# Products with v for two slots at once, tails' scores in four quadrants, and a gate and a spatial product ordered by their stationary operand

## The chip, the cores and the metric

The program runs on one core of a Trainium2 chip (trn2). The metric is the device time of one execution in microseconds (us). A profile of one execution goes with it. Its engines are PE (matrix products, with PEld for the loads of their stationary operands), DVE (vector), ACT (scalar functions), POOL and SP; SP here only starts DMA transfers. Each engine takes its instructions in the order in which the program lists them.

## What is computed

Attention with rotary position, then a channel mixing block, then a gated block with a spatial product. Cut to what matters (B, H, S, D = 4, 8, 576, 64; DM = 512, DF = 1024):

```python
scores = matmul(rotate(q), rotate(k).T) / sqrt(D)             # per batch and head, 576 x 576
attn = exp(scores - max); attn /= attn.sum() + 1e-9
x = concat_heads(matmul(attn, v))                             # [B, 576, 512]
xk, xr = mix of x and x shifted by one row, with mu_k and mu_r
v2 = square(relu(xk @ w_k)) @ w_v
x = sigmoid(xr @ w_r) * v2
h = relu(x @ w_in); u, g = h[..., :512], h[..., 512:]
g = (g - mean(g)) / sqrt(var(g) + 1e-6)
out = (u * (w_spatial @ g + b_spatial)) @ w_out
```

## The kernel before, in words

Products in fp32 precision are sums of three products of high and low parts (a high times w high, a low times w high, a high times w low) in a type that PE takes in one pass; only the scores are plain fp32, which PE runs as two passes (two records in the trace for each product of the program). The weights with the low parts arrive as 64-bit numbers and are taken apart on ACT, DVE and POOL.

**The first part** (to about 502 us, with a tail that overlaps the second part) is attention and the first block. It is cut into 72 slots, 18 for each batch. A pair is two heads, 64 rows of q and k each, one in partitions 0 to 63 and one in 64 to 127 (`HEAD[0]`, `HEAD[1]`). Slot m of a batch takes 128 queries of one pair (16 slots), or the last 64 queries of two pairs: these are the tails, slots 8 and 9 of a batch. A slot goes through these steps:

- `scores` (line 318, PE): for two halves h of the 576 keys and two heads j, 128 x 288 products into two tiles `ps[0]`, `ps[1]` of PSUM, of which there is one set more. In a tail, pair u = 0 is done first, then u = 1; head j writes partitions `HEAD[j]` of `ps[u]`.
- `top` (L324, DVE), twice: the maximum of a row. `expo` (L329, ACT), twice: the exponential with its sum. `norm` (L334, L335, DVE).
- `high` (L341, ACT) and `low` (L345, DVE), twice each: the probabilities as two fp16 parts, into the tile `p16` (named `p` in the trace), of which there are 3 (`P16S`).
- `turn` (L350, issued by SP): a DMA that transposes `p16` into a tile `pt`, of which there are 3 (`PTS`).
- `values` (L370, PE): 9 pieces of 128 keys, two parts of v, two heads: 36 products of 64 columns of v with 128 queries, the two heads in the two column halves of PE (partitions `HEAD[j]` of one PSUM bank `pv`). A tail has 72 products with 64 queries each.
- `gather` (ACT) copies a `pv` bank out after slots 3, 7, 9, 13 and 17 of a batch, and so makes the input of the block that follows.

For the queries before and after row 256 of each batch the first block runs as `k_dot` (L432, named `mk`), `k_square` and `v_dot` (L462, named `mv`). `prep` loads q, k and v of the next pairs and rotates them (`rope`, L225 and L226, DVE).

The order of this part is made by `Plan`: each step is added with a rank, an engine, a price in us and the steps and buffers that it needs; the planner walks through them and writes, for each engine, the order in which they are issued. The order on the chip is fixed by that, also where a step then waits.

**The second part** (from 502 us) runs batch by batch: `receptance` (product `r`), `gate` (product `hv`, whose stationary operand is the part `x[a]`, 12 products of 512 columns for each 128 rows), `branch` (product `u`, whose stationary operand is the weight), `spatial` (product `sp`, whose stationary operand is the part `vn[a]`) and `project` (product `o`). In `product` each stationary operand is used for two products of 288 columns. `PARTS = (0, 0), (1, 0), (0, 1)` is the order of the parts as (part of the activation, part of the weight). The scheduler of the framework orders this part.

Of the kernel before, what the change touches and what calls it, by code (L numbers as in the profile page):

```python
# [30 lines left out]
RAW, ROT, VVS, PFS, P16S, PTS = 2, 8, 4, 4, 3, 3  # L31
# [65 lines left out]
def body(ctx: ExitStack, tc, qp, kp, vp, cs, mu_k, mu_r, w_k, w_v, w_r, w_in, w_sp, b_sp, w_out, out):  # L97
# [209 lines left out]
    def scores(m):  # L307
        ps = [ps_s.tile([128, 2, 512], F32, tag="s", name=f"s{n}")
              for n in (2 * m, 2 * m + 1)]
        w = which(m)  # L310
        for u in range(2 if w[0][2] == 64 else 1):
            i, c, n, _ = w[u]
            q, k = preps[i][0], preps[i][1]
            for h in range(2):
                for j in range(2):
                    r = HEAD[j]
                    o = ps[u][r, h, :HALF] if n == 64 else ps[j][:, h, :HALF]
                    nc.tensor.matmul(o, q[r, c:c + n], k[r, h * HALF:(h + 1) * HALF], start=True, stop=True)  # L318
        sm = at.tile([128, 4, 2], F32, tag="sm", bufs=4, name=f"sm{m}")
        units[m] = [[x[:, :, :HALF] for x in ps], sm, [None, None], None]  # L320
# [26 lines left out]

    def turn(m):
        pt = at.tile([128, 2, NKC, 128], F16, tag="pt", bufs=PTS, name=f"pt{m}")
        nc.sync.dma_start_transpose(pt.rearrange("p u c q -> p (u c) q"),  # L350
                                    units[m][3].rearrange("p u a b -> p (u a b)"))
        units[m] = pt
# [3 lines left out]
    def values(m):  # L356
        b, w = divmod(m, UN)
        pt = units.pop(m)
# [77 lines left out]
    def k_square(b, h, fc):  # L436
        ps = mo.pop((b, h, "k", fc))[:, :PART[h][1]]
        if fc % 2 == 0:
            mo[b, h, "s"] = moe_tile([128, 2, PART[1][1]], F32, "rl", 2, name=f"rl{b}_{h}_{fc}")[:, :, :PART[h][1]]
        rl = k2 = mo[b, h, "s"]  # L440
# [35 lines left out]
    def moe1(b, h):  # L476

        end = UN * b + (20 if h else 10)
        s, places = end + 1.6, 16 if h else 20
# [18 lines left out]
        for fc in range(NFC):  # L498
            m = at_(fc)
            bank, q, r = ("m", P, fc), fc // 2, ("rl", P, fc // 2)  # L500
            for k in range(2):
                add(m + .1 * k, "PE", .9 * f, lambda fc=fc, k=k: k_dot(b, h, fc, k), ("k", P, fc, k),
                    needs=[("x3", P, 2 * k), ("x3", P, 2 * k + 1)] + [("wlo", c + 4 * (fc // 4)) for c in (2 * k, 2 * k + 1)]
                    + ([("k", P, fc, 0)] if k else last if fc > 3 else []), take=[] if k else [("m", bank)],
                    use=[("x", P)] + ([bank] if k else []))
# [9 lines left out]
        for dc, half in ((0, 0), (1, 0), (0, 1), (1, 1), (2, 0), (2, 1), (3, 0), (3, 1)):  # L515
            m = at_(8 + n)
            n += 1
            for k in (2 * half, 2 * half + 1):
                add(m + .1 * (k % 2), "PE", .9 * f, lambda dc=dc, k=k: v_dot(b, h, dc, k), ("v", P, dc, k),
# [14 lines left out]
    for m in range(N):  # L534
# [3 lines left out]
        add(m - .5, "PE", 1.17, lambda m=m: scores(m), ("s", m), needs=[("rope", *r) for r in rots] + [("s", m - 1)][:m],  # L538
            use=[("rot", *r) for r in rots], take=[("s", ("s", m, 0)), ("s", ("s", m, 1)), ("sm", ("sm", m))])
        for j in range(2):  # L540
            add(m - .4 + .01 * j, "DVE", .71, lambda m=m, j=j: top(m, j), ("top", m, j), needs=[("s", m)], use=[("s", m, j)])
# [9 lines left out]
            needs=[("low", m, 0), ("low", m, 1)] + [("turn", m - 1)][:m], use=[("p16", m)],  # L551
            take=[("pt", ("pt", m))], dma=3.4)
        first = w in (0, 4, 8, 10, 14)
        if first:
            bank = ("pvb", m)
        add(m + 1.5, "PE", 1.15, lambda m=m: values(m), ("pv", m),
            needs=[("turn", m)] + [("vcopy", i) for i in pairs] + ([("pv", m - 1)] if m else []),
            use=[("pt", m)] + [("vv", i) for i in pairs] + ([] if first else [bank]), take=[("pvb", bank)] if first else [])
# [54 lines left out]
    PARTS = (0, 0), (1, 0), (0, 1)  # L613

# [78 lines left out]
    def gate_rows(name, x, c):  # L693
# [3 lines left out]
        for d in range(NP):  # L697
            for a, w in PARTS:
# [155 lines left out]
```

## Time and profile before

| | us |
|---|---|
| median of 3 runs (818.06 to 820.53) | 819.29 |
| the execution that was profiled | 818.47 |
| its span, first to last instruction | 816.7 |
| PE busy in the span | 716.5 (88%) |
| DVE busy | 548.4 (67%) |
| ACT busy | 487.0 (60%) |
| DMA queue of SP, share of 16 engines | 58.0% |

The span is read by stretches, since different engines set the pace in different ones: one row of the windows view for each stretch gives the busy time of each engine in it, with the count of instructions behind the x, then the clock granted to PE (1.00 is 2.4 GHz, 0.50 is 1.2 GHz) and the mean busy share of the 16 DMA engines. In the chain of waits, each row is a start, a duration and the instructions on the path that ended last, so many (x) of them.

### The profile page before, as it was taken

What the parts mean: (1) busy time and instruction counts of PE and PEld (TensorE: products, weight loads), DVE (VectorE), ACT (ScalarE), POOL (GpSimd) and SP (SyncE); (2) the same over time, 40 slices, a digit from 0 to 9 for tenths busy, and PEclk for the clock granted to TensorE, in tenths of its full rate; (3) what the DMA queues carried; (4) which work ended last, traced back from release to release, by engine and by line L of the source; (5) the groups of instructions that cost most, each with busy time, mean ns of one, the idle gap of its engine ahead of it and who ended that gap; (6) DMA issues with size and microseconds to landing.
All of it is one profiled execution on the core that took longest, in us unless ns stands there. A gap on an engine that the chain in (4) does not pass through costs nothing.

```text
span 816.7 us, 16914 instructions
## 1 busy us (share of the span) xinstructions
PE 716.5 (88%) x6872; PEld 622.7 (76%) x6872; DVE 548.4 (67%) x935; ACT 487.0 (60%) x980; POOL 107.8 (13%) x171
## 2 busy tenths in 40 slices
PE   2267698779999689998899997978899999999997
PEld 1144477558888568897688887977899999998997
DVE  4997999877589887689975664768756232635211
ACT  2657877569678488577695886876633412523311
POOL 0214312111001010001110001351301000201000
PEclk9975889969999889999799999998999999999999
DMA  7879987888589967699986767567210302010101
GB/s 252 248 174 192 248 198 133 201 175 147 148 192 210 209 129 160 134 210 218 180 140 126 127 126 191 164 202 243 59 59 1 117 8 96 29 31 1 59 1 59
DMA packets 197552, 114.19 MB, mean 140 GB/s; under 512 B 172961, under 2 KB 177057, under 8 KB 197474
## 3 DMA queue, kind: packets, MB, share of 16 engines
q1 hardware_dynamic: 195794, 107.79, 58.0%
q0 software_dynamic: 1536, 4.73, 1.8%
q8 instruction: 54, 0.88, 0.4%
q10 hardware_dynamic: 144, 0.59, 0.2%
q14 instruction: 24, 0.20, 0.1%
HBM read 52.26 MB, written 14.16 MB: 81 GB/s over the span
## 4 chain that ended last, share of the span: by engine, by line
PE 50%; DVE 4%; ACT 4%; DMA 4%; issue 1%; POOL 0%; DVEq 0%; ACTq 0%; SPq 0%
PE sp L625 7%; PE mv L462 6%; PE mk L432 6%; PE o L625 6%; PE s L318 5%; PE hv L699 5%; PE r L625 5%; PE u L625 5%; PE pv L370 4%; DMA pt<-p 1%; DMA I-8206_8207<-w_sp 1%; DMA I-8247_8248<-w_out 1%; DMA I-7579_7580<-w_in 1%; DMA I-7623_7624<-w_in 1%; DVE sm L324 1%
## 5 line engine op out<-in xcount | busy, mean ns | idle before, releaser
L318 PE MATMUL s<-rot,rot 64*128 64x288 f32 (+1 forms) x640 | 129.1, 481 | 55.6 <-ACT pf L329 41.9
L329 ACT ACTIVATE pf<-s,sm 128x576 f32<-128x576 f32 x144 | 106.2, 739 | 58.7 <-DVE sm L324 57.9
L318 PEld LDWEIGHTS s<-rot,rot 64*128 64x128 f32 (+1 forms) x640 | 66.9, 199 | 91.9 <-ACT pf L329 55.9
L432 PE MATMUL mk<-x,wk 128*128 128x256 f32 (+1 forms) x768 | 121.0, 307 | 12.0 <-ACT x L420 7.1
L341 ACT ACTIVATE p<-pf,sm 128x576 f16<-128x576 f32 x144 | 109.4, 771 | 36.6 <-DVE sm L335 17.5
L324 DVE TENSOR_REDUCE sm<-s 128x1 f32<-128x576 f32 x144 | 107.0, 751 | 34.9 <-PE s L318 34.6
L345 DVE SCALAR_TENSOR_TENSOR p<-pf,sm,p 128x576 f16<-128x576 f32 x144 | 118.9, 833 | 17.2 <-ACT p L341 17.1
L432 PEld LDWEIGHTS mk<-x,wk 128*128 128x128 f32 x768 | 107.3, 193 | 25.0 <-ACT x L420 7.9
L462 PE MATMUL mv<-kk,wv 128*128 128x256 f32 (+1 forms) x768 | 117.9, 302 | 1.5 <-DVE kk L450 1.5
L370 PEld LDWEIGHTS <-vv 128*64 128x64 f16 x2880 | 89.1, 122 | 36.6 <-issue 30.0
L462 PEld LDWEIGHTS mv<-kk,wv 128*128 128x128 f32 x768 | 104.8, 189 | 14.1 <-issue 10.3
L370 PE MATMUL pv<-pt,vv 128*64 128x128 f16 (+1 forms) x2880 | 100.1, 232 | 17.0 <-DMA pt<-p 16.9
L625 PE MATMUL r<-xr,wr 128*128 128x288 f32 x384 | 55.6, 302 | 2.7 <-DVE xr L629 2.1
L625 PEld LDWEIGHTS r<-xr,wr 128*128 128x128 f32 x384 | 53.6, 194 | 3.8 <-DVE xr L629 2.6
L699 PE MATMUL hv<-wi,x 128*128 128x512 f32 x192 | 48.7, 402 | 6.9 <-ACT x L628 6.7
L625 PE MATMUL sp<-ws,vn 128*128 128x288 f32 x384 | 53.9, 295 | 0.0
L625 PE MATMUL u<-x,wi 128*128 128x288 f32 x384 | 53.6, 298 | 0.0
L625 PEld LDWEIGHTS u<-x,wi 128*128 128x128 f32 x384 | 52.8, 190 | 1.0
L625 PE MATMUL o<-g,wo 128*128 128x288 f32 x384 | 53.0, 296 | 0.5 <-ACT os L755 0.5
L625 PEld LDWEIGHTS sp<-ws,vn 128*128 128x128 f32 x384 | 52.4, 188 | 0.7
L625 PEld LDWEIGHTS o<-g,wo 128*128 128x128 f32 x384 | 51.7, 188 | 1.4 <-ACT os L755 1.2
L699 PEld LDWEIGHTS hv<-wi,x 128*128 128x128 f32 x192 | 35.9, 192 | 14.7 <-ACT x L628 6.9
(293 smaller groups left out, 836.6 us busy)
## 6 DMA issues: line engine op xcount, KB each, us to landing
raw<-kp SPq DMA_DIRECT2D x15, 576.0 KB, 4.7
raw<-qp SPq DMA_DIRECT2D x15, 576.0 KB, 4.5
vr<-vp SPq DMA_DIRECT2D x16, 320.0 KB, 3.8
v<-vd SPq DMA_DIRECT2D x16, 288.0 KB, 2.9
out<-os SPq DMA_DIRECT2D x16, 288.0 KB, 2.1
vv<-vv SPq DMA_DIRECT2D x32, 128.0 KB, 3.2
x<-xd SPq DMA_DIRECT2D x12, 288.5 KB, 3.2
xd<-xt POOLq DMA_DIRECT2D x16, 160.0 KB, 4.5
```

Of the source, the lines that this page charges most:

```text
L318: nc.tensor.matmul(o, q[r, c:c + n], k[r, h * HALF:(h + 1) * HALF], start=True, stop=True)
L324: nc.vector.tensor_reduce(sm[:, 0, j:j + 1], ps[j], axis=AX.XY, op=ALU.max, negate=True)
L329: nc.scalar.activation(pf[j].rearrange("p (a b) -> p a b", a=2), ps[j], AF.Exp, bias=sm[:, 0, j:j + 1], scale=1.0, accum_out=sm[:, 1, j:j ...
L341: nc.scalar.mul(p16[:, j, 0, :], pf[j], sm[:, 3, j:j + 1])
L345: nc.vector.scalar_tensor_tensor(p16[:, j, 1, :], pf[j], sm[:, 3, j:j + 1], p16[:, j, 0, :], op0=ALU.mult, op1=ALU.subtract)
L370: nc.tensor.matmul(pv[HEAD[j], o:o + n], preps[i]["vv"][:, kc, j, D * hl:D * hl + D], a, start=kc + hl == 0, stop=kc + hl == NKC)
L432: nc.tensor.matmul(ps[:, :PART[h][1]], wk[c][fc // 4][:, w, fc % 4 * 128:fc % 4 * 128 + 128], a[:, c, :], start=m == 0, stop=m == 11)
L462: nc.tensor.matmul(ps[:, :PART[h][1]], wv[fc][:, w, dc * 128:(dc + 1) * 128], a, start=m == 0, stop=m == 23)
L625: nc.tensor.matmul(ps[:, h, :HALF], w, a[:, h * HALF:(h + 1) * HALF], start=m == 0, stop=m == n - 1)
L699: nc.tensor.matmul(ps[:, :FS], x[a][:, d, c:c + 128], wi[w][:, d, FS:], start=k == 0, stop=k == 11)
```

## The change

- `values` now runs once for two slots (m even and m + 1), after both transposes: 36 products with 256 queries each in place of 72 with 128. The slots of a pair share one tile `pt`, twice as large; there are 2 of them (`PTS` 3 to 2, which is 4 slots' room in place of 3). The pair of tails is done in one call, with 144 products of 64 queries as before.
- `p16` has 2 buffers in place of 3 (`P16S`).
- In a tail's `scores` the halves of the keys are the outer loop, and head j of pair u writes partitions `HEAD[j ^ u]`: four products in a row take the four combinations of 64 rows and 64 columns of PE.
- `gate` and `spatial` take the parts in the order `FIRST = (0, 0), (0, 1), (1, 0)`, so that products with the same stationary part follow each other.
- In the planner: `top` has rank m - 1.4 (was m - .4), `values` rank m + 2.5 with price 2.2, `scores` price 1.24 (was 1.17), `k_dot` and `v_dot` price .94 (was .9), and the first block's places start at end + 2 (was end + 1.6). `k_square` names its buffer by pair of tiles.

```diff
-RAW, ROT, VVS, PFS, P16S, PTS = 2, 8, 4, 4, 3, 3
+RAW, ROT, VVS, PFS, P16S, PTS = 2, 8, 4, 4, 2, 2
...
-        for u in range(2 if w[0][2] == 64 else 1):
-            i, c, n, _ = w[u]
-            q, k = preps[i][0], preps[i][1]
-            for h in range(2):
+        for h in range(2):
+            for u in range(2 if w[0][2] == 64 else 1):
+                i, c, n, _ = w[u]
+                q, k = preps[i][0], preps[i][1]
                 for j in range(2):
                     r = HEAD[j]
-                    o = ps[u][r, h, :HALF] if n == 64 else ps[j][:, h, :HALF]
+                    o = ps[u][HEAD[j ^ u], h, :HALF] if n == 64 else ps[j][:, h, :HALF]
...
     def turn(m):
-        pt = at.tile([128, 2, NKC, 128], F16, tag="pt", bufs=PTS, name=f"pt{m}")
+        if m % 2 == 0:
+            pts[m // 2] = at.tile([128, 2, 2, NKC, 128], F16, tag="pt", bufs=PTS, name=f"pt{m}")
+        pt = pts[m // 2][:, m % 2]
...
-        for us in ((0,), (1,)) if w in (8, 9) else ((0, 1),):
+        for k, u in [(k, u) for k in range(2) for u in range(2)] if w == 8 else [(0, None)]:
             for kc in range(NKC):
                 for hl in range(2):
                     for j in range(2):
-                        u = us[j % len(us)]
-                        i, _, n, o = which(m)[u]
-                        a = pt[:, u, kc, HEAD[j]] if n == 64 else pt[:, u, kc, :]
+                        if u is None:
+                            i, _, n, o = which(m)[0]
+                            a, n = pt[:, :, j, kc, :], 256
+                        else:
+                            i, _, n, o = which(m + k)[u]
+                            a = pt[:, k, u, kc, HEAD[j ^ u]]
...
-            for a, w in PARTS:
+            for a, w in FIRST:
                 nc.tensor.matmul(ps[:, :FS], x[a][:, d, c:c + 128], wi[w][:, d, FS:], start=k == 0, stop=k == 11)
...
-            product(ps, [(vn[a][:, c, sl], ws[w][:, c, :]) for c in range(4) for a, w in PARTS]
+            product(ps, [(vn[a][:, c, sl], ws[w][:, c, :]) for c in range(4) for a, w in FIRST]
```

Three places show what stands in the engines' orders.

PE at the first tail, before: the end of a `values` call (loads of v, products with 128 queries), then the tail's scores, four products for one tile and four for the other (64x288), then the first block:

```order
L370 LDWEIGHTS vv_360
L370 MATMUL pv_630<-pt_541,vv_360 64x128
L318 MATMUL s_675<-rot_1_131,rot_0_134 64x288 x4
L318 MATMUL s_676<-rot_1_184,rot_0_204 64x288 x4
L432 MATMUL mk_0_0_706<-x_0_0_598,wk_98 128x256
```

And now:

```order
L319 MATMUL s_522<-rot_1_334,rot_0_411 128x288
L319 MATMUL s_564<-rot_1_131,rot_0_134 64x288 x2
L319 MATMUL s_565<-rot_1_184,rot_0_205 64x288 x2
L319 MATMUL s_564<-rot_1_131,rot_0_134 64x288 x2
L319 MATMUL s_565<-rot_1_184,rot_0_205 64x288 x2
L378 LDWEIGHTS vv_337
L378 MATMUL pv_589<-pt_455,vv_337 64x256
```

The tail's products alternate between the two tiles by twos, and the products with v take 256 queries.

DVE in the last batch, slots 65 to 67 (`sm` the sums and maxima of a slot, `s` a tile of scores, `pf` the exponentials, `p` the fp16 parts), before:

```order
L334 TENSOR_SCALAR sm_6401<-sm_6401 128x2
L335 RECIPROCAL sm_6401<-sm_6401 128x2
L324 TENSOR_REDUCE sm_6471<-s_6465 128x1
L345 SCALAR_TENSOR_TENSOR p_6475<-pf_0_6425,sm_6401,p_6475 128x576
L324 TENSOR_REDUCE sm_6471<-s_6466 128x1
L345 SCALAR_TENSOR_TENSOR p_6475<-pf_1_6453,sm_6401,p_6475 128x576
L450 TENSOR_TENSOR kk_0_1_6550<-rl_0_0_6451,kk_0_1_6550 128x2x256
```

And now:

```order
L335 TENSOR_SCALAR sm_5267<-sm_5267 128x2
L336 RECIPROCAL sm_5267<-sm_5267 128x2
L325 TENSOR_REDUCE sm_5320<-s_5314 128x1
L325 TENSOR_REDUCE sm_5320<-s_5315 128x1
L346 SCALAR_TENSOR_TENSOR p_5323<-pf_0_5289,sm_5267,p_5323 128x576
L346 SCALAR_TENSOR_TENSOR p_5323<-pf_1_5299,sm_5267,p_5323 128x576
L335 TENSOR_SCALAR sm_5320<-sm_5320 128x2
```

Both maxima of the next slot now stand ahead of both low parts of this one.

PE in the first gate (`x20_0` the high and `x20_1` the low part, the stationary operand; `wi0`, `wi1` the weight's parts), before:

```order
L699 MATMUL hv0_0_7798<-wi0_7466,x20_0_7698 128x512
L699 MATMUL hv0_1_7821<-wi0_7466,x20_0_7698 128x512
L699 MATMUL hv0_2_7844<-wi0_7466,x20_0_7698 128x512
L625 MATMUL u0_0_7890<-x20_0_7698,wi0_7466 128x288 x2
L625 MATMUL u0_1_7917<-x20_0_7698,wi0_7466 128x288 x2
L699 MATMUL hv0_0_7798<-wi0_7466,x20_1_7699 128x512
L699 MATMUL hv0_0_7798<-wi1_7467,x20_0_7698 128x512
```

And now:

```order
L712 MATMUL hv0_0_6610<-wi0_6278,x20_0_6510 128x512
L712 MATMUL hv0_0_6610<-wi1_6279,x20_0_6510 128x512
L712 MATMUL hv0_1_6633<-wi0_6278,x20_0_6510 128x512
L712 MATMUL hv0_1_6633<-wi1_6279,x20_0_6510 128x512
L712 MATMUL hv0_2_6656<-wi0_6278,x20_0_6510 128x512
```

The two products with the high part now follow each other.

## Rows read from the trace of the kernel before

**Rows 1.** The page: busy us, share, instructions; granted PE clock by slice.

```profile
PE 716.5 (88%) x6872; PEld 622.7 (76%) x6872; DVE 548.4 (67%) x935; ACT 487.0 (60%) x980; POOL 107.8 (13%) x171
PEclk9975889969999889999799999998999999999999
```

**Rows 2.** Busy time by stretch; then the granted clock, DMA share and GB/s.

```profile
20.00:180.00 160.00, 109.94 (x1151) 80.28 (x1150) 145.50 (x231) 110.06 (x229) 37.69 (x45) 0.82 0.87 197
180.00:260.00 80.00, 80.00 (x987) 68.36 (x986) 61.13 (x108) 60.44 (x134) 4.88 (x15) 0.99 0.80 172
260.00:297.00 37.00, 27.61 (x288) 21.40 (x288) 30.34 (x59) 22.77 (x49) 4.60 (x8) 0.82 0.79 171
297.00:380.00 83.00, 83.00 (x1010) 70.56 (x1011) 65.57 (x114) 62.02 (x138) 7.51 (x19) 1.00 0.87 172
380.00:405.00 25.00, 20.12 (x214) 13.83 (x212) 23.28 (x43) 17.29 (x37) 3.51 (x5) 0.82 1.01 217
405.00:502.00 97.00, 94.78 (x1232) 81.95 (x1228) 61.38 (x116) 69.55 (x156) 5.77 (x16) 0.99 0.75 134
502.00:572.00 70.00, 58.69 (x362) 55.62 (x363) 52.23 (x72) 54.85 (x99) 23.55 (x20) 0.93 0.64 205
572.00:817.00 245.00, 237.47 (x1630) 227.74 (x1628) 99.43 (x180) 85.00 (x138) 18.69 (x38) 0.99 0.13 43
```

**Rows 3.** The same view for line 370 alone: PE busy (x), PEld busy (x).

```profile
180.00:260.00 80.00, 15.81 (x540) 13.81 (x540) 0.99 0.80 172
297.00:380.00 83.00, 15.81 (x540) 13.81 (x540) 1.00 0.87 172
405.00:502.00 97.00, 22.29 (x720) 19.78 (x716) 0.99 0.75 134
```

**Rows 4.** Chain of waits, 305 to 345 us: start, duration, work.

```profile
314.78 1.13 PE pv L370 x36
317.86 2.09 PE s L318 x16
332.98 1.17 PE s L318 x8
```

**Rows 5.** Timeline of PE, windows 317.80 to 317.83 and 318.09 to 318.12.

```profile
317.80 0.46 PE L318 MATMUL s<-rot,rot 64*64 64x288 f32 x2
317.80 0.70 PE L318 MATMUL s<-rot,rot 64*64 64x288 f32 x4
```

**Rows 6.** Timeline of PE at the end of attention; in brackets its wait.

```profile
488.19 1.24 PE L318 MATMUL s<-rot,rot 64*128 64x288 f32 x8
...
498.19 1.20 PE L370 MATMUL pv<-pt,vv 128*64 128x128 f16 x36 [1.18 <-DMA pt<-p]
499.32 1.15 PE L432 MATMUL mk<-x,wk 128*128 128x320 f32 x6
500.75 1.20 PE L370 MATMUL pv<-pt,vv 128*64 128x128 f16 x36 [0.28 <-DMA pt<-p]
```

**Rows 7.** Timelines of ACT and SP (slots 48 to 50); landing times of line 350, 340 to 400 us.

```profile
353.38 0.77 ACT L341 ACTIVATE p<-pf,sm 128x576 f16<-128x576 f32 x1
360.38 1.44 ACT L341 ACTIVATE p<-pf,sm 128x576 f16<-128x576 f32 x2
367.00 0.78 ACT L341 ACTIVATE p<-pf,sm 128x576 f16<-128x576 f32 x1
360.26 5.37 SPq L350 DMA_TRANSPOSE pt<-p  x1
DMA to landing us min/median/max: 4.6/6.7/9.0
```

**Rows 8.** Chain of waits, 600 to 670 us.

```profile
606.67 7.47 PE hv L699 x32
639.66 12.80 PE u L625 x96
652.46 14.92 PE sp L625 x112
```

More of the change, by code (lines that the diff above doesn't have):

```diff
@@ L346, in low @@
                                        op1=ALU.subtract)
+    pts = {}
     def turn(m):
-        pt = at.tile([128, 2, NKC, 128], F16, tag="pt", bufs=PTS, name=f"pt{m}")
+        if m % 2 == 0:
+            pts[m // 2] = at.tile([128, 2, 2, NKC, 128], F16, tag="pt", bufs=PTS, name=f"pt{m}")
+        pt = pts[m // 2][:, m % 2]
         nc.sync.dma_start_transpose(pt.rearrange("p u c q -> p (u c) q"),
-                                    units[m][3].rearrange("p u a b -> p (u a b)"))
-        units[m] = pt
+                                    units.pop(m)[3].rearrange("p u a b -> p (u a b)"))
     pvt = {}
@@ L357, in values @@
         b, w = divmod(m, UN)
-        pt = units.pop(m)
+        pt = pts.pop(m // 2)
         if w in (0, 4, 8, 10, 14):
@@ L438, in k_square @@
         if fc % 2 == 0:
-            mo[b, h, "s"] = moe_tile([128, 2, PART[1][1]], F32, "rl", 2, name=f"rl{b}_{h}_{fc}")[:, :, :PART[h][1]]
-        rl = k2 = mo[b, h, "s"]
+            mo[b, h, "s", fc // 2] = moe_tile([128, 2, PART[1][1]], F32, "rl", 2, name=f"rl{b}_{h}_{fc}")[:, :, :PART[h][1]]
+        rl = k2 = mo[b, h, "s", fc // 2]
         nc.scalar.activation(rl[:, fc % 2, :], ps, AF.Relu)
@@ L478, in moe1 @@
         end = UN * b + (20 if h else 10)
-        s, places = end + 1.6, 16 if h else 20
+        s, places = end + 2, 16 if h else 20
         at_ = lambda m: s + .5 * (m * places / 16)
@@ L501, in moe1 @@
             for k in range(2):
-                add(m + .1 * k, "PE", .9 * f, lambda fc=fc, k=k: k_dot(b, h, fc, k), ("k", P, fc, k),
+                add(m + .1 * k, "PE", .94 * f, lambda fc=fc, k=k: k_dot(b, h, fc, k), ("k", P, fc, k),
                     needs=[("x3", P, 2 * k), ("x3", P, 2 * k + 1)] + [("wlo", c + 4 * (fc // 4)) for c in (2 * k, 2 * k + 1)]
@@ L518, in moe1 @@
             for k in (2 * half, 2 * half + 1):
-                add(m + .1 * (k % 2), "PE", .9 * f, lambda dc=dc, k=k: v_dot(b, h, dc, k), ("v", P, dc, k),
+                add(m + .1 * (k % 2), "PE", .94 * f, lambda dc=dc, k=k: v_dot(b, h, dc, k), ("v", P, dc, k),
                     needs=[("kl", P, k), ("wlo", 8 + 2 * k), ("wlo", 9 + 2 * k)] + ([("v", P, dc, k - 1)] if k else []),
@@ L537, in body @@
         rots = [(i, a) for i in pairs for a in range(2)]
-        add(m - .5, "PE", 1.17, lambda m=m: scores(m), ("s", m), needs=[("rope", *r) for r in rots] + [("s", m - 1)][:m],
+        add(m - .5, "PE", 1.24, lambda m=m: scores(m), ("s", m), needs=[("rope", *r) for r in rots] + [("s", m - 1)][:m],
             use=[("rot", *r) for r in rots], take=[("s", ("s", m, 0)), ("s", ("s", m, 1)), ("sm", ("sm", m))])
         for j in range(2):
-            add(m - .4 + .01 * j, "DVE", .71, lambda m=m, j=j: top(m, j), ("top", m, j), needs=[("s", m)], use=[("s", m, j)])
+            add(m - 1.4 + .01 * j, "DVE", .71, lambda m=m, j=j: top(m, j), ("top", m, j), needs=[("s", m)], use=[("s", m, j)])
             add(m - .3 + .01 * j, "ACT", .93, lambda m=m, j=j: expo(m, j), ("exp", m, j), needs=[("top", m, j)],
@@ L550, in body @@
         add(m + .7, "SP", .1, lambda m=m: turn(m), ("turn", m),
-            needs=[("low", m, 0), ("low", m, 1)] + [("turn", m - 1)][:m], use=[("p16", m)],
-            take=[("pt", ("pt", m))], dma=3.4)
+            needs=[("low", m, 0), ("low", m, 1)] + [("turn", m - 1)][:m], use=[("p16", m)] + [("pt", m // 2)] * (m % 2),
+            take=[] if m % 2 else [("pt", ("pt", m // 2))], dma=3.4)
         first = w in (0, 4, 8, 10, 14)
@@ L555, in body @@
             bank = ("pvb", m)
-        add(m + 1.5, "PE", 1.15, lambda m=m: values(m), ("pv", m),
-            needs=[("turn", m)] + [("vcopy", i) for i in pairs] + ([("pv", m - 1)] if m else []),
-            use=[("pt", m)] + [("vv", i) for i in pairs] + ([] if first else [bank]), take=[("pvb", bank)] if first else [])
+        if m % 2 == 0:
+            both = sorted({*pairs, *(u[0] for u in which(m + 1))})
+            add(m + 2.5, "PE", 2.2, lambda m=m: values(m), ("pv", m + 1),
+                needs=[("turn", m), ("turn", m + 1)] + [("vcopy", i) for i in both] + ([("pv", m - 1)] if m else []),
+                use=[("pt", m // 2)] + [("vv", i) for i in both] + ([] if first else [bank]),
+                take=[("pvb", bank)] if first else [])
         if w in (3, 7, 9, 13, 17):
@@ L613, in body @@
     PARTS = (0, 0), (1, 0), (0, 1)
+    FIRST = (0, 0), (0, 1), (1, 0)
     def two_bank(ps):
```

## The prediction

> **What bounds the kernel now.** I read the page first: PE is busy for 716.5 of 816.7 us, DVE for 548.4, and the granted clock dips in the first half [rows 1]. An 88% share says little for a program of several parts, so the next view is busy time by stretch [rows 2]. The reader is to see three kinds. In 180 to 260, 297 to 380 and 405 to 502 PE is busy for 80.00 of 80, 83.00 of 83 and 94.78 of 97 us, at a clock of 0.99 or 1.00 (the 2.4 GHz level), with DVE at 61.13, 65.57 and 61.38: there a shorter PE step shortens the program. In 20 to 180, 260 to 297 and 380 to 405 DVE is the fuller engine (145.50 of 160, 30.34 of 37, 23.28 of 25) and PE stands idle for 50, 9 and 5 us: a shorter PE step is worth nothing there. From 572 on PE is the bound again (237.47 of 245), with other products. What lies between, 502 to 572, is a chain that starts when attention has ended, and moves with that end.
>
> All sums are against the profiled execution, 818.47 us (span 816.7, 1.8 outside it). The median of the runs is 0.8 above it, and I add that at the end. About 0.3%, 2.5 us, is what a measurement of this kernel can tell from no change.
>
> **Products with v.** A call of `values` takes 1.13 us for 36 products of 128 queries [rows 4]. Two heads go to the two column halves, so that is 18 couples of 62.8 ns. At 2.4 GHz 128 columns are 53.3 ns; some 9.4 ns a couple, or 0.17 us a call, are entry and spacing. A couple of 256 queries streams 106.7 ns; with the same overhead the new call takes 18 x 116.1 ns = 2.09 us, against 2 x 1.13 = 2.26: **0.17 us less for two slots**. The bounds: no overhead at all gives 1.92 us (0.34 less); the pace of the fp32-like products, 14.92 us for 112 of 288 columns [rows 8] or 0.463 ns a column, gives 18 x 118.5 + 0.12 = 2.25 (nothing gained). I take 0.17, since it comes from the same operation. It counts only where PE is full. There 540 + 540 + 720 = 1800 products run [rows 3]; six of the tails lie there, with 72 each, which leaves 1368, or 38 slots, or 19 pairs: 19 x 0.17 = **-3.2 us** (0 to -6.5). The tails' own products with v stay as they are, 64 queries each.
>
> **Scores of the tails.** A tail takes 2.09 us for 16 records, a usual slot 1.17 for 8 [rows 4], so a step of two records costs (2.09 - 1.17) / 4 = 0.23 us. Two records start together: within 30 ns of the start the timeline has 2 of them, and 0.3 us later the next 2 have begun [rows 5]; these are the two heads, on different rows and columns. A tail is thus 8 steps of two. Now four products in a row take four different quadrants. If all four overlap, a tail has 4 steps and costs 1.17 us, 0.92 less. If the second couple starts one step after the first, because it uses the same rows, some 5 steps are left: 1.40 us, 0.69 less. Before, no fp32 products on equal rows and different columns ran side by side; the nearest row is the products with v, whose two column halves use the same rows and do overlap (62.8 ns for two of 53.3 each) [rows 4]. So I take the middle, 0.80. Of the eight tails six lie where PE is full [rows 3]: 6 x 0.80 = **-4.8 us** (0 to -5.5).
>
> The Trainium skill, page "TensorE: Matmul & The Clock Gate", section "Part 3: Packing small matmuls", has a rule against this: loads of stationary operands overlap with products in flight only when they are for other rows. By it the second couple, on the same rows, would wait, the tail would stay near 2.09 us, and the sum would be without this term. The trace does not agree for the products with v, whose halves share all rows; for fp32 no run shows it yet.
>
> **The end of attention.** In the last batch PE waits for transposes: 1.18 and 0.28 us ahead of the last two `values` [rows 6], since the last slot's scores start at 488.19 and its transpose has landed only at 500.7, 12.5 us later. In the new order 14 pieces of `v_dot` (6 products of 256 columns, 0.71 us at the 0.463 ns a column of [rows 8]), the second last pair (2.09) and two pieces of `k_dot` (6 of 320 columns, 0.89) stand between the last scores and the last pair, 13.8 us in all, so that the wait is covered. A piece of `k_dot` that stood ahead of the last `values` (at 499.32 in [rows 6]) now stands behind it: 0.89. Together 1.18 + 0.28 + 0.89 = **-2.3 us**; at worst the last pair adds its second half to the chain, +1.
>
> **What the pairs wait for.** The even slot of a pair now waits for the odd slot's transpose. Odd slots keep their place, three slots of scores behind, so most of the wait stays covered by first-block products; I add what the trace shows for such waits in 405 to 502, 1.18 + 0.28, rounded: **+1.5 us** (0 to 19 x 1.18 = 22 if every pair waited as the worst one did). Behind a waiting `values` PE holds back the scores of the next slot, and DVE the maximum of those.
>
> **Edits at nothing.** Both maxima ahead of the low parts on DVE: one of the two low parts starts 0.75 us later, the second at the same time, and the transpose needs both. In the DVE-full stretches the work of DVE is the same in amount: 0, bounded by their idle time, 14.5 + 6.7 + 1.7 = 23 us, on the side of gain. Gate and spatial product by stationary operand: `u` already runs with equal stationary operands up to four in a row (its weight is used for both activation parts), `sp` before changes every two, and both take 133 ns a product (12.80 / 96 and 14.92 / 112) [rows 8]; `hv` takes 233 ns for 512 columns. Order is therefore worth nothing: 0, within 1 us either way. The 1152 products fewer save no DVE, ACT or DMA work; transposes and loads are the same in number.
>
> **Sum.** -3.2 - 4.8 - 2.3 + 1.5 = -8.8. 818.47 - 8.8 = 809.7, and 0.8 for the median: **810.5 us**, 1.1% faster.
>
> **The rivals.**
>
> *Two buffers of p16 set the pace (slower).* A buffer is taken when `high` starts and is free when its transpose has landed. Slot 48 took it at 353.38; its transpose was issued at 360.26 and took between 6.7 (median there) and 9.0 us to land [rows 7], so it was held for 13.6 to 15.9. Slot 50 began `high` at 367.00 and so needed a third one, or came within a fraction of a microsecond of it. With two buffers a slot takes at least 6.8 to 7.9 us, 7.35 in the middle, against 6.6 between slots 49 and 50 [rows 7]: 0.75 a slot. If ACT stands there, everything behind `high` stands, `expo` of the next slot and the copies of the first block among it. In 20 to 180 and 297 to 405, where the DMA share is 0.87 to 1.01 [rows 2], lie some 35 slots, 26 us if all are paced so; with half of that the result is 823.5. Against it speaks that SP's order is made for two buffers now (transposes stand further ahead of the stores), that DVE work stands between the low parts of a slot and the `high` of two slots later, and that in 405 to 502 the DMA share is 0.75. It decides from 8.8 / 35 = 0.25 us a slot.
>
> *The quadrants don't overlap.* By the rule above the tails stay at 2.09 us: 810.5 + 4.8 = 815.3. [Rows 4] speak against it, and [rows 5] show nothing of it.
>
> *DVE takes what PE gives up.* If the PE-full stretches turn out to be paced by the loop of scores, maximum, exponential and low part, only the last one (no rotation for a next batch there) gains: a third of 8.0 and the 2.3, so 818.47 - 2.7 - 2.3 + 0.8 = 814.3. DVE's 25% of idle time there [rows 2] speaks against it.
>
> *The DVE-full stretches gain too.* With maxima first, scores come earlier and DVE waits less; half of the 23 us idle is 11, so 799.5. DVE at 91% in the longest of them leaves little room.
>
> **How the numbers follow.** Chances: the forecast 0.42, two buffers 0.22, quadrants 0.08, DVE 0.16, the fast case 0.12. The forecast's own bounds from the terms are 804 to 816. Range: from 801, which leaves out about half of the fast case, to 822, which leaves out about half of the two-buffer case. Faster by over 0.3% (below 816.8): the forecast, the fast case, most of the quadrant case and two thirds of the DVE case, 0.72, less some for the odds that several small waits add up: 0.70. Slower: most of the two-buffer case, 0.18. The same: 0.12.
>
> **What would show it.** In the profile after: a `values` call of 36 records at 2.05 to 2.15 us in the chain; a tail's scores at 1.2 to 1.4 us; PE without idle time ahead of the last pair; `u` and `sp` still at 133 ns, `hv` at 233; the stretch from the first product of `u` to the end as long as before. Two buffers would show as waits of `high` (L342) for the transpose, near zero in a right forecast, and as DVE waits for ACT. Waits of `values` for the transpose of over 5 us in the PE-full stretches would make the prediction wrong, as would PE no longer being full in them.

## The result, and the profile after

The changed kernel took **803.31 us** (median of 4 runs, 802.47 to 808.04) beside 819.42 for the kernel before (4 runs): a ratio of 0.9827, 95% interval 0.9803 to 0.9851. The forecast was 810.5 with a range of 801 to 822, so sign and range held; of the 16.1 us gained it had seen 8.8. The profiled execution took 803.87 us (span 802.1), 14.6 less than the profiled one of before. One execution each of e3 and of e11 below stands near 835 us with a granted clock of 0.82 over the whole run; both are left out of the numbers, and nothing is read from the traces of these two.

The page of the kernel after (busy us, share, instructions; granted clock by slice), to be read against [rows 1]:

```profile
PE 699.4 (87%) x5720; PEld 608.3 (76%) x5720; DVE 548.7 (68%) x935; ACT 484.7 (60%) x980; POOL 108.7 (14%) x171
...
PEclk9996769989999989999799999989999999999999
```

PE is busy for 17.1 us less, DVE and ACT about as long as before. To see where the span lost its 14.6 us, both kernels are cut at the start of the last product with v of each batch. The windows view of the kernel before (from:to, length, then busy time of PE, PEld, DVE, ACT and POOL with their counts, granted clock, DMA share, GB/s):

```profile
0.00:172.90 172.90, 110.33 (x1121) 80.06 (x1122) 150.69 (x240) 110.06 (x226) 37.61 (x48) 0.86 0.86 204
172.90:284.60 111.70, 103.28 (x1262) 87.36 (x1258) 85.73 (x153) 79.36 (x172) 9.59 (x23) 0.94 0.84 181
284.60:400.80 116.20, 107.99 (x1270) 88.04 (x1266) 95.53 (x171) 84.25 (x183) 11.02 (x24) 0.94 0.86 174
400.80:501.70 100.90, 98.52 (x1245) 83.81 (x1242) 64.76 (x123) 73.42 (x163) 7.32 (x19) 0.97 0.74 133
501.70:816.70 315.00, 296.40 (x1999) 283.44 (x1993) 151.66 (x251) 139.87 (x236) 42.25 (x57) 0.98 0.25 79
```

The same five stretches of the kernel after; its last line answers to the last full stretch of [rows 2]:

```profile
0.00:176.20 176.20, 106.68 (x834) 75.87 (x834) 149.87 (x239) 108.94 (x225) 40.37 (x49) 0.86 0.83 202
176.20:285.10 108.90, 101.98 (x980) 84.98 (x976) 91.47 (x164) 82.87 (x180) 10.13 (x24) 0.95 0.90 185
285.10:394.00 108.90, 101.69 (x980) 84.14 (x978) 92.43 (x164) 82.08 (x180) 10.33 (x24) 0.97 0.92 188
394.00:488.50 94.50, 92.28 (x944) 79.75 (x940) 61.41 (x117) 71.83 (x159) 6.67 (x17) 0.96 0.69 135
488.50:802.10 313.60, 296.77 (x2002) 283.60 (x1996) 153.49 (x251) 138.94 (x236) 41.20 (x57) 0.98 0.25 80
...
405.00:488.50 83.50, 83.50 (x890) 73.20 (x886) 53.75 (x101) 62.54 (x139) 5.01 (x13) 1.00 0.70 135
```

By length the five changed by +3.3, -2.8, -7.3, -6.4 and -1.4 us. The gain lies in the second to fourth batch, where PE is the fuller engine: of -16.5 us there, PE's busy time makes -13.8 (309.79 before, 295.95 after) and its idle time -2.7 (19.0 to 16.35). The first batch, where DVE is the fuller engine, gained nothing; it is longer. Up to the end of attention PE stays full (83.50 of 83.5).

The products themselves, in the chain of waits of the kernel after, 305 to 345 us (start, duration, work), against [rows 4]:

```profile
317.38 1.13 PE s L319 x16
322.23 2.09 PE pv L378 x36
324.31 1.17 PE s L319 x8
```

The products with v of two slots take 2.09 us, and a tail's 16 records of scores 1.13, where they took 2.09. PE's timeline of the kernel after, window 317.31 to 317.34, is to be read against [rows 5]: there two records had started within 30 ns, here four.

```profile
317.31 0.47 PE L319 MATMUL s<-rot,rot 64*64 64x288 f32 x4
```

The waits of PE (engine, line, what is waited for: us in total, times, longest), first of the kernel before, then of the kernel after, and of ACT after:

```profile
PE pv L370 <- DMA pt<-p: 16.9, 11, 2.8
```

```profile
PE s L319 <- ACT pf L330: 47.0, 23, 6.9
...
PE pv L378 <- DMA pt<-p: 2.5, 4, 1.0
...
ACT p L342 <- DMA pt<-p: 16.5, 15, 2.4
```

PE waits less for transposes than before, 2.5 us against 16.9. In the second and third batch together they fell from 10.5 to 2.0 us, while the waits of the scores for the exponentials rose from 3.8 to 8.6. `high` does wait for the two buffers of `p16`, 15 times and 16.5 us in all, where the kernel before has one such wait of 3.7 us. In one place the chain of waits of the kernel after runs through it (there `high` waited 1.44 us):

```profile
257.85 17.02 DMA pt<-p x2
274.89 0.78 ACT p L342
```

The end of attention, PE's timeline of the kernel after (start, duration, work), against [rows 6]:

```profile
471.11 1.24 PE L319 MATMUL s<-rot,rot 64*128 64x288 f32 x8
472.28 5.30 PE L470 MATMUL mv<-kk,wv 128*128 128x256 f32 x42
477.51 2.16 PE L378 MATMUL pv<-pt,vv 128*64 128x256 f16 x36
...
486.58 2.15 PE L378 MATMUL pv<-pt,vv 128*64 128x256 f16 x36
488.67 1.14 PE L440 MATMUL mk<-x,wk 128*128 128x320 f32 x6
```

Neither of the last two `values` has a wait behind it in brackets, and a piece of `k_dot` follows the last one. The second part runs at its old pace; the chain of the kernel after, 585 to 660 us, against [rows 8]:

```profile
586.22 0.70 PE hv L712 x3
586.92 2.22 PE sp L638 x17
...
592.08 7.47 PE hv L712 x32
...
625.07 12.80 PE u L638 x96
637.87 14.92 PE sp L638 x112
```

### The profile page after: what moved, and what is told of

The parts are those of the page before. It is cut to its first block, busy times and chain, and to the rows that moved or that the text cites. A ratio compares the mean times of both kernels' runs of the same rounds, so it can differ in the third digit from the quotient of the medians.

```text
span 802.1 us, 14609 instructions
## 1 busy us (share of the span) xinstructions
PE 699.4 (87%) x5720; PEld 608.3 (76%) x5720; DVE 548.7 (68%) x935; ACT 484.7 (60%) x980; POOL 108.7 (14%) x171
## 4 chain that ended last, share of the span: by engine, by line
PE 57%; DVE 22%; DMA 10%; ACT 6%; issue 4%; POOL 1%; SPq 0%; DVEq 0%; ACTq 0%; POOLq 0%
PE mk L440 8%; PE mv L470 7%; PE sp L638 7%; PE pv L378 7%; PE s L319 7%; PE o L638 6%; DMA pt<-p 6%; PE hv L712 5%; PE u L638 5%; PE r L638 5%; DVE p L346 5%; DVE sm L325 4%; DVE raw L225 3%; DMA vr<-vp 2%; ACT pf L330 1%
## 5 line engine op out<-in xcount | busy, mean ns | idle before, releaser
L319 PE MATMUL s<-rot,rot 64*128 64x288 f32 (+1 forms) x640 | 121.6, 485 | 72.6 <-ACT pf L330 47.0
L319 PEld LDWEIGHTS s<-rot,rot 64*128 64x128 f32 (+1 forms) x640 | 62.9, 198 | 110.3 <-ACT pf L330 63.1
L440 PE MATMUL mk<-x,wk 128*128 128x256 f32 (+1 forms) x768 | 122.8, 313 | 11.5 <-DVE x L430 6.9
L440 PEld LDWEIGHTS mk<-x,wk 128*128 128x128 f32 x768 | 110.1, 199 | 26.8 <-issue 10.1
L346 DVE SCALAR_TENSOR_TENSOR p<-pf,sm,p 128x576 f16<-128x576 f32 x144 | 117.2, 829 | 19.2 <-ACT p L342 18.8
L325 DVE TENSOR_REDUCE sm<-s 128x1 f32<-128x576 f32 x144 | 104.3, 751 | 31.5 <-PE s L319 31.4
L342 ACT ACTIVATE p<-pf,sm 128x576 f16<-128x576 f32 x144 | 108.5, 770 | 24.8 <-DMA pt<-p 16.5
L470 PE MATMUL mv<-kk,wv 128*128 128x256 f32 (+1 forms) x768 | 112.9, 300 | 1.8 <-DVE kk L458 1.8
L378 PE MATMUL pv<-pt,vv 128*64 128x256 f16 (+1 forms) x1728 | 89.4, 265 | 2.6 <-DMA pt<-p 2.5
L378 PEld LDWEIGHTS <-vv 128*64 128x64 f16 x1728 | 77.2, 119 | 18.6 <-issue 11.4
L638 PE MATMUL r<-xr,wr 128*128 128x288 f32 x384 | 53.9, 296 | 3.7 <-DVE xr L642 2.4
```

The costliest lines, as they stand in the source:

```text
L325: nc.vector.tensor_reduce(sm[:, 0, j:j + 1], ps[j], axis=AX.XY, op=ALU.max, negate=True)
L342: nc.scalar.mul(p16[:, j, 0, :], pf[j], sm[:, 3, j:j + 1])
L346: nc.vector.scalar_tensor_tensor(p16[:, j, 1, :], pf[j], sm[:, 3, j:j + 1], p16[:, j, 0, :], op0=ALU.mult, op1=ALU.subtract)
L440: nc.tensor.matmul(ps[:, :PART[h][1]], wk[c][fc // 4][:, w, fc % 4 * 128:fc % 4 * 128 + 128], a[:, c, :], start=m == 0, stop=m == 11)
L470: nc.tensor.matmul(ps[:, :PART[h][1]], wv[fc][:, w, dc * 128:(dc + 1) * 128], a, start=m == 0, stop=m == 23)
L638: nc.tensor.matmul(ps[:, h, :HALF], w, a[:, h * HALF:(h + 1) * HALF], start=m == 0, stop=m == n - 1)
```

## The experiments

Each ratio is to the kernel before on the same chip, with its 95% interval; times are medians. The kernel before took 818.4 us beside e1 to e4, 818.7 beside e5 to e8 and 817.95 beside e9 to e12. So two runs of different groups are better compared by their ratios than by their times.

| | what differs | us | ratio |
|---|---|---|---|
| after | | 803.31 | 0.9827 (0.9803 to 0.9851) |
| e1 | after, order of the parts as before | 804.13 | 0.9819 (0.9779 to 0.9859) |
| e2 | after, tails' scores as before | 809.37 | 0.9891 (0.9855 to 0.9927) |
| e3 | after, products with v 128 queries wide | 807.05 | 0.9848 (0.9790 to 0.9907) |
| e4 | after, old rank of `top` | 803.26 | 0.9808 (0.9761 to 0.9856) |
| e5 | before, with the quadrants | 816.0 | 0.9960 (0.9938 to 0.9981) |
| e6 | before, with the pairs | 813.88 | 0.9932 (0.9906 to 0.9957) |
| e7 | after, all old numbers in the planner | 813.15 | 0.9929 (0.9905 to 0.9953) |
| e8 | before, with the new numbers | 809.89 | 0.9880 (0.9850 to 0.9909) |
| e9 | after, first block priced .90 | 827.15 | 1.0103 (1.0068 to 1.0138) |
| e10 | after, first block priced .98 | 810.3 | 0.9896 (0.9864 to 0.9928) |
| e11 | after, old places of the first block | 806.41 | 0.9853 (0.9813 to 0.9893) |
| e12 | after, scores priced 1.17 | 806.82 | 0.9867 (0.9830 to 0.9905) |

### e1: the order by stationary operand

```diff
-    FIRST = (0, 0), (0, 1), (1, 0)
+    FIRST = PARTS
```

> The changed kernel with the gate and the spatial product back in the old order of parts; nothing else differs. Theory (order by stationary operand is worth nothing, since u and sp both took 133 ns a product before): 803.3 us, within 1. Rival (equal stationary operands in a row save their loads, or the low part is needed later and the first gate starts earlier): 2 to 6 us more, 805 to 809, with hv above 234 ns or sp above 134 ns a product.

Measured: 804.13 us, ratio 0.9819, not to be told from the changed kernel's 0.9827 (the interval is 3.3 us to either side). In its chain `u` takes 12.80 us for 96 and `sp` 14.92 for 112, as in both other kernels. With each product at its old pace, the order by stationary operand is worth nothing here.

### e2: the quadrants taken out

```diff
-        for h in range(2):
-            for u in range(2 if w[0][2] == 64 else 1):
+        for u in range(2 if w[0][2] == 64 else 1):
+            for h in range(2):
...
-                    o = ps[u][HEAD[j ^ u], h, :HALF] if n == 64 else ps[j][:, h, :HALF]
+                    o = ps[u][r, h, :HALF] if n == 64 else ps[j][:, h, :HALF]
```

> The changed kernel with the tails' scores on the two diagonal quadrants alone, in the old order of loops; the planner's order is the same. Theory (four quadrants overlap fully, 0.92 us a tail, and six of the eight tails lie where PE is full): 803.3 + 5.5 = 808.8 us, 810.7 if all eight count. Rival (the gain of the tails is taken by waits that follow, since the maxima of a tail can now start only when both tiles are done): under 2 us more, below 805.5.

Measured: 809.37 us, 6.1 more than with the quadrants by the times and 5.2 by the ratios. Its chain, 305 to 345 us, has the tail at its old length, with all else of the order as in the changed kernel:

```profile
309.67 2.09 PE s L319 x16
312.83 2.09 PE pv L378 x36
```

Against 1.13 us that is 0.96 for each tail, and six tails where PE is full make 5.8, the whole difference within its noise. The forecast had taken 0.80.

### e3: the pair's products narrow again, in the same place

```diff
-        for k, u in [(k, u) for k in range(2) for u in range(2)] if w == 8 else [(0, None)]:
+        for k, u in [(k, u) for k in range(2) for u in range(2)] if w == 8 else [(0, None), (1, None)]:
...
-                            a, n = pt[:, :, j, kc, :], 256
+                            a = pt[:, k, j, kc, :]
```

> The changed kernel with the products with v of a pair of slots done as 72 of 128 queries in place of 36 of 256, at the same place in the order. Theory (width alone is worth 0.17 us a pair, less one entry of 0.12 that this kernel keeps saving): a pair takes 2.14 us where it took 2.09, so 0.05 x 32 = 1.6 us at most, 803.3 to 805. Rival (each couple of 128 queries costs its full 62.8 ns, 2.26 us a pair): 0.17 x 22 to 32 pairs = 3.7 to 5.4 more, 807 to 809.

Measured: 801.41, 807.05 and 809.68 us. The interval of the ratio, 0.9790 to 0.9907, holds both theories; the run is inconclusive.

### e4: the maxima late again

```diff
-            add(m - 1.4 + .01 * j, "DVE", .71, lambda m=m, j=j: top(m, j), ("top", m, j), needs=[("s", m)], use=[("s", m, j)])
+            add(m - .4 + .01 * j, "DVE", .71, lambda m=m, j=j: top(m, j), ("top", m, j), needs=[("s", m)], use=[("s", m, j)])
```

> The changed kernel with the rank of the row maxima as before (m - .4), everything else as changed; the planner's order changes on all engines with it. Theory (what was gained beyond the forecast, some 7 us, comes from the maxima that now stand ahead of the low parts, so that scores come earlier in the stretches that DVE fills): about 810 us. Rival (it comes from the pairs and the two p16 buffers, or from the tails' full overlap): within 2 us of 803.3.

Measured: 803.26 us. The 810 us of the theory lie outside the interval (0.9761 to 0.9856 of 818.4, or 799 to 807), so the rank of the maxima is not where the surplus comes from.

### e5 and e6: the two edits alone, in the kernel before

e5 puts the two lines of e2, turned round, into the kernel before, with its old numbers. e6 puts the pairs there (one `values` for two slots, two `pt`, two `p16`), without quadrants, and keeps the old numbers but for the rank and price that the joint call needs:

```diff
-RAW, ROT, VVS, PFS, P16S, PTS = 2, 8, 4, 4, 3, 3
+RAW, ROT, VVS, PFS, P16S, PTS = 2, 8, 4, 4, 2, 2
...
-        add(m + 1.5, "PE", 1.15, lambda m=m: values(m), ("pv", m),
+            add(m + 2.5, "PE", 2.2, lambda m=m: values(m), ("pv", m + 1),
```

> The kernel before with the tails' scores in four quadrants and nothing else; the planner's order is that of before. Theory (0.92 us a tail, six of eight where PE is full, the two others hidden by DVE): 5.5 us less than before, 813 to 814. Rival (all eight count, 7.4 less): 812. Second rival (a shorter tail only lengthens the wait for the next step): within 2 us of before.

> The kernel before with the products with v for two slots at once (with 2 buffers of p16 and 2 of the double pt), old ranks and prices, the tails and the gate as before. Theory of the forecast (3.2 less for the width, 2.3 less at the end, 1.5 more for waits): 4 us less than before, 814 to 815.5. Rival (the pairs carry the gain that the forecast lacked, by fewer changes between kinds of products on PE and a looser order): 7 to 10 us less, 809 to 812. Second rival (two p16 buffers cost what the pairs bring when the planner's numbers are old): no gain, 817 to 821.

Measured: 816.0 us for e5, 2.7 less than before, half of what e2 showed in the other direction; 813.88 for e6, 4.8 less. Both signs are as forecast. Of the 5.5 us that the theory gave e5, half arrives, although a tail's scores take 1.13 us in its chain too; where the rest goes was not read. The 4.8 of e6 are the size that its theory gave, but not in its place: in its profiled execution the first batch is 9.5 us shorter than before (163.4), and the second to fourth, where the pairs should gain, are 5.2 longer (334.0 against 328.8 together), with PE busy at 1.2 GHz for 35.2 us in place of 25.5 (counted from the clock's intervals and PE's records). So the size came out by luck.

### e7 and e8: the planner's numbers, both ways

e7 is the changed kernel with all five old numbers; e8 is the kernel before with the five new ones and no other edit (but `k_square`'s names). Three of the five, in e8:

```diff
-        s, places = end + 1.6, 16 if h else 20
+        s, places = end + 2, 16 if h else 20
...
-                add(m + .1 * k, "PE", .9 * f, lambda fc=fc, k=k: k_dot(b, h, fc, k), ("k", P, fc, k),
+                add(m + .1 * k, "PE", .94 * f, lambda fc=fc, k=k: k_dot(b, h, fc, k), ("k", P, fc, k),
...
-        add(m - .5, "PE", 1.17, lambda m=m: scores(m), ("s", m), needs=[("rope", *r) for r in rots] + [("s", m - 1)][:m],
+        add(m - .5, "PE", 1.24, lambda m=m: scores(m), ("s", m), needs=[("rope", *r) for r in rots] + [("s", m - 1)][:m],
```

> The changed kernel with all ranks and prices of the planner as before (maxima, first block's places, scores, k_dot and v_dot); pairs, quadrants and gate as changed. Theory (the numbers are worth nothing beyond scatter, the gain comes from the products themselves): within 2 us of the changed kernel, 801 to 806. Rival (they carry the 7 us beyond the forecast): 808 to 812.

> The kernel before with the planner's new ranks and prices alone, with 3 buffers of p16 and of pt, tails and products with v as before. Theory (worth nothing): within 2 us of before, 817 to 821. Rival (they carry the 7 us): 811 to 814.

Measured: the edits alone bring 5.6 us (818.7 to 813.15), the numbers alone 8.8 (to 809.89), and together they bring 16.1. By the ratios the numbers are worth 8.4 to 9.8 us and the edits 4.3 to 5.8. That the numbers are worth nothing, which the forecast had taken without a word, fell. Two windows rows of e7 (second and third batch), to be read against those of the kernel after above:

```profile
165.50:282.10 116.60, 105.84 (x978) 87.43 (x976) 94.99 (x170) 83.26 (x180) 12.22 (x25) 0.91 0.88 179
282.10:396.50 114.40, 103.80 (x981) 87.59 (x976) 91.54 (x165) 82.18 (x178) 9.89 (x24) 0.93 0.83 177
```

The same products keep PE busy 3.9 and 2.1 us longer, at a clock of 0.91 and 0.93 (after: 0.95 and 0.97), and leave it idle 3.8 and 3.4 us longer. In the first batch e7 is 10.7 us shorter than the kernel after (165.5), so the loss in the others is not all loss. The windows of e8, first and second batch:

```profile
0.00:164.30 164.30, 110.73 (x1120) 81.84 (x1122) 145.69 (x232) 107.08 (x223) 38.40 (x46) 0.82 0.88 211
164.30:280.00 115.70, 105.04 (x1274) 87.69 (x1268) 95.05 (x174) 84.47 (x185) 11.47 (x26) 0.95 0.88 180
```

Here the gain over the kernel before is in the first batch, 8.6 us, and the second is 4.0 longer. The new numbers thus gain a similar amount in both kernels, but in different batches; no one mechanism for it is seen.

### e9 to e12: one number at a time

e9 and e10 move the price of a piece of the first block, e11 puts its places back, e12 the price of the scores. One of the two lines of e9, the other is the same for `v_dot`:

```diff
-                add(m + .1 * k, "PE", .94 * f, lambda fc=fc, k=k: k_dot(b, h, fc, k), ("k", P, fc, k),
+                add(m + .1 * k, "PE", .9 * f, lambda fc=fc, k=k: k_dot(b, h, fc, k), ("k", P, fc, k),
```

> The changed kernel with one number of the planner put back: a piece of the first block (k_dot, v_dot) is priced at .9 in place of .94. If one number carries the 10 us by which the kernel with all old numbers was slower, and it is this one (in the trace such a piece takes 0.72 to 0.89 us, 1.08 after a change of products, so .94 stands nearer to its true length), this run takes 810 to 814 us. If the 10 us belong to no single number, and each set of numbers gives another order with its own scattered cost, it lands anywhere from 802 to 812, with no relation to the step of the price. If this number is without effect, 802 to 804.5.

> The changed kernel with the same price moved the other way, to .98. If the price works by its size (a higher price leaves more room for the scores, maxima and exponentials between the pieces), the time keeps falling or stands still: 800 to 804. If it is scatter between orders, this run is slower than the changed kernel like its neighbours, 804 to 812, since the changed kernel's set of numbers would be the best of several.

> The changed kernel with the first block's places from end + 1.6 as before, in place of end + 2. With values called a pair at a time, and so up to one slot later, a place that is .4 slots too early puts pieces of the first block on PE that wait for the copies of that pair's bank. If that carries the 10 us: 810 to 814, with longer waits of PE for ACT ahead of k_dot than in the changed kernel. If another number carries it: 802 to 804.5. If it is scatter: anywhere from 802 to 812.

> The changed kernel with the scores priced at 1.17 as before, in place of 1.24. A slot's scores do take 1.17 us in the trace, so that the higher price only moves one piece of the first block in some 13 slots. If it carries the 10 us: 810 to 814. If another number does: 802 to 804.5. If it is scatter: anywhere from 802 to 812.

Measured: 827.15, 810.3, 806.41 and 806.82 us. By the price the time goes 827, 803, 810 for .90, .94 and .98, so a price that works by its size falls, and so does one number that carries the 10 us: e9 loses 24, more than all five old numbers together in e7. The intervals of e11 and e12 overlap with that of the changed kernel; e9, e10 and e7 are told apart from it. What is left, argued and not shown, is that each set of numbers is another order with its own cost, and even that theory had expected at most 812.

One place in e9 can be read. Its waits between 378 and 392 us, PE's and ACT's:

```profile
PE mk L440 <- ACT vs L477: 4.1, 1, 4.1
...
ACT vs L477 <- DMA vd<-vs: 4.9, 1, 4.9
```

The timeline of e9 around it (start, duration, work; SPq is SP's queue; in brackets the idle time before and what ended it):

```profile
374.71 6.74 SPq L355 DMA_TRANSPOSE pt<-p  x1
377.76 0.37 ACT L477 COPY vs<-mv 128x256 f32<-128x256 f32 x1
...
382.18 5.55 SPq L482 DMA_DIRECT2D vd<-vs  x3
386.52 0.65 ACT L477 COPY vs<-mv 128x256 f32<-128x256 f32 x2 [4.92 <-DMA vd<-vs]
```

SP stands at a transpose for 6.74 us and waits for DVE (line 430, by the list of waits). Behind it stand the stores of the first block's copies `vs`, of which the last was made at 378.13 (377.76 + 0.37); they are issued only from 382.18. ACT needs their buffer for its next copy and waits 4.92 us, with the exponentials behind it; PE waits 4.06 us for ACT. Then the clock falls, as the windows of e9 show:

```profile
365.00:385.00 20.00, 17.89 (x154) 15.16 (x153) 19.69 (x36) 13.68 (x31) 1.93 (x4) 1.00 0.87 184
385.00:406.00 21.00, 15.91 (x106) 11.81 (x106) 13.78 (x24) 9.90 (x19) 0.94 (x2) 0.70 0.73 158
```

At 0.70 some 60% of the stretch ran at 1.2 GHz, and neither PE (15.9 of 21) nor DVE (13.8) was full. The kernel after has a weak place at the same point, though. There PE never waits for line 477, but it stands 3.26 us for the exponentials, and the clock falls as well; its timeline and its windows:

```profile
386.82 0.99 PE L319 MATMUL s<-rot,rot 64*128 64x288 f32 x2 [3.26 <-ACT pf L330]
```

```profile
385.00:394.00 9.00, 6.78 (x42) 4.56 (x44) 7.22 (x14) 4.51 (x9) 0.38 (x1) 0.62 1.01 185
394.00:410.00 16.00, 13.78 (x94) 10.86 (x91) 10.90 (x21) 12.35 (x26) 1.66 (x4) 0.79 0.69 136
```

The third batch of e9 is 10.4 us longer than that of the kernel after (119.3 against 108.9): 5.1 of it are idle time of PE (12.3 against 7.2) and 5.3 busy time (107.0 against 101.7), with PE busy at 1.2 GHz for 17.8 us in place of 6.4. From 365 us to the batch's end PE is idle for 7.2 us in e9 and for 3.7 in the kernel after, so the wait for the store makes only a part of the 10.4; and the batch is only a part of the 18.1 us between the two profiled spans. The profiled execution of e9, 821.95 us, is also the fastest of its six. What the rest of the 24 us is stays open.

## Why the prediction was right, and where it was not

**What bounds the kernel** held. The gain of PE's time shows where PE was full, and the batch in which DVE is fuller gave none of it.

**Products with v.** The call is 2.09 us, as worked out, so a pair of slots does save the 0.17. The term of -3.2 was too small all the same. It counted the 19 pairs of the stretches in which PE is full, where the three batches have 24, and it put at nothing what the calls cost the products beside them. PE's timeline of the kernel before shows that:

```profile
336.05 1.20 PE L370 MATMUL pv<-pt,vv 128*64 128x128 f16 x36
337.17 1.15 PE L462 MATMUL mv<-kk,wv 128*128 128x320 f32 x6
338.25 1.24 PE L318 MATMUL s<-rot,rot 64*128 64x288 f32 x8
339.42 1.15 PE L462 MATMUL mv<-kk,wv 128*128 128x320 f32 x6
340.41 0.88 PE L432 MATMUL mk<-x,wk 128*128 128x256 f32 x6
341.12 1.04 PE L462 MATMUL mv<-kk,wv 128*128 128x320 f32 x6
342.01 0.88 PE L432 MATMUL mk<-x,wk 128*128 128x256 f32 x6
```

From start to start, six products of `mv` take 0.89 us between two runs of `mk` (341.12 to 342.01), 0.99 between scores and `mk` (339.42 to 340.41) and 1.08 between `values` and scores (337.17 to 338.25). So a run of the first block's products takes 0.10 us more when a run of attention's products stands ahead of it and 0.09 more when one follows. A call of `values` takes 1.12 to 1.13 whatever stands beside it, so this comes on top of the call's own time. Counted along PE's records, such borders in the second to fourth batch fell from 152 to 106; 46 times 0.09 to 0.10 is an estimate of 4.1 to 4.6 us at 2.4 GHz, which the forecast lacked. That the block's products got shorter is seen in `mv` alone, in the windows of the second batch before and after, for the same 192 products, all of them at 2.4 GHz by the clock's intervals:

```profile
172.90:284.60 111.70, 29.91 (x192) 0.94 0.84 181
176.20:285.10 108.90, 28.33 (x192) 0.95 0.90 185
```

**Scores of the tails.** Here the term was -4.8 at 0.80 a tail, and the chain shows 0.96, -5.8. The reason for the middle, that products on equal rows might start one step late, is what failed: all four quadrants run side by side, as e2 shows (6.1 us for this edit alone).

**The end of attention** went as worked out: there is no wait ahead of the last two calls (1.46 gained), and `k_dot` stands behind the end (0.89).

**What the pairs wait for.** Forecast +1.5; in fact PE's waits for transposes fell (16.9 to 2.5 us), and all idle time of PE in the three batches by 2.7, the 1.46 of the end among it. This step had the wrong sign by some 2.7 us in all.

Put together for the second to fourth batch: PE's records, each counted from its start to the next one's without idle time, give 67.0 us before and 62.7 after for `values` (-4.3), 169.7 and 166.4 for the first block's products (-3.3), and 73.1 and 66.9 for scores (-6.2). Together that is the measured -13.8. Of the -4.3, 24 pairs at 0.17 make 4.0, and the tails' calls, which run as one for two, the rest. Of the -3.3, 0.9 is the piece of `k_dot` that moved behind the end, and 2.4 remain of the 4.1 to 4.6 of the borders; these products spent 4.8 us at 1.2 GHz in place of 1.7, which took some of it back. Of the -6.2 the quadrants make 5.8. With the idle time, -2.7, the first batch, +3.3, and what follows attention, -1.4, the account closes at -14.6.

**What the sum left out** is the larger point. The change sets five numbers anew in the planner, and the prediction gave them no term. By e7 and e8 they are worth 8 to 10 us and the edits 4 to 7. That sign and range held is thus partly luck: more than half of the 16.1 us came by a way that the forecast did not see, and with the old numbers its terms bring no time in the batches where it had placed them. The account above holds for this order, but the PE time that the edits save reaches the end only with it. In e7 the same edits leave the second to fourth batch at 116.6, 114.4 and 98.5 us, 329.5 together, against 328.8 for the kernel before: the saved work was given back as PE time at 1.2 GHz (38.2 us busy in place of 25.5; a slot's scores take 2.22 us there and 1.17 at 2.4 GHz, so half of the difference, 6.4, is an estimate of the loss) and idle time (24.9 in place of 19.0), and the gain of e7 came from a shorter first batch (165.5 against 172.9). Why one set of numbers leaves shorter waits at the ends of batches than another is read for one place of e9 alone; beyond that it stays open. Of the seven sets run with the edits complete (803.3, 803.3, 806.4, 806.8, 810.3, 813.2 and 827.2) the changed kernel has the best or ties with it, and the median, 806.8, is nearer to the forecast's 810.5 than the changed kernel is.

**The rivals.** Two buffers of `p16` are seen: the prediction wanted waits of `high` near zero, and they are 16.5 us. They don't pace 35 slots at 0.75 us each, as the rival had it, since the second to fourth batch got shorter, but one such wait lies on the chain; no run gives the changed kernel three buffers, so what they cost is not shown. That quadrants don't overlap is refuted by the chain and e2. DVE did not take the gain: PE is still full up to the end of attention, and its time there is shorter. The fast case was near in time (799.5) but not in place: the first batch, the longest stretch in which DVE is fuller, grew. Order by stationary operand, forecast at nothing, is shown to be nothing by e1, and so is the rank of the maxima by e4.

## What to carry to other kernels

Where an order written ahead rules the engines, price the new order too: changes of the planner's numbers moved this kernel by up to 24 us, 3%, with the same work. A forecast from saved work alone leaves that out, and two neighbouring sets of numbers should be timed before an edit is judged. Count how often an engine changes its kind of work, not only the work; a joint call also shortens what stands beside it. When an order turns out slow, a store or copy queued behind an instruction that waits (here SP's transpose) is one place to look; look at the same place in the faster order too before it is called the cause.

## What the runs showed of the hardware

- A run of products on the whole of PE (128x128) takes 0.10 us more behind products on 64 columns or 64 rows, and 0.09 more ahead of them, in both kernels. Between `mv` and `mk` or `hv` and `sp`, all 128x128, a change costs nothing: in the chain above 3 products of `hv` among `sp` take 0.70 us, and 32 of them 7.47, both 0.233 each. The Trainium skill, page "TensorEngine Tiling (Array Packing)", section "Key Properties", says that a change of the tiling mode drains TensorE; the trace agrees in where the cost falls. That the drain is its cause is not shown, since the operands change with the tiling and no run changes one of them alone.
- Four fp32 products in the four quadrants of PE, two and two on equal rows, overlap fully: 16 records in 1.13 us, where two at a time took 2.09 (e2). The rule of the Trainium skill that the prediction weighed (page "TensorE: Matmul & The Clock Gate", "Part 3: Packing small matmuls"), that loads overlap with products only on other rows, does not hold for this pattern; the measurement decides.
- The one-pass products of the fp32 sums keep 133 ns for 288 columns and 233 ns for 512 whichever of the operands is repeated (e1 and the chain above).
